# Another order for the opening of an attention-then-FFN kernel: v cast, copies, phis and transposes moved between engines

## The chip, the cores and the metric

The kernel runs on one core of one Trainium2 chip. The time is device microseconds of one execution, from start to end; a verdict is made on the median of several executions. TensorE (PE) multiplies, VectorE (DVE), ScalarE (ACT) and GpSimd (POOL) work elementwise, and SyncE (SP) issues most of the loads and stores. GpSimd also issues the DMAs that cast the weights to bf16 on their way in. Each engine works through its own instructions in the order written.

## The reference

```python
# attention: q, k, v are (8, 8, 576, 64) float32
theta = np.pi / 2.0 * pos / S
phi(x) = concatenate([relu(x) * cos(theta), relu(x) * sin(theta)])   # 64 -> 128
kv  = einsum('bhsf,bhsd->bhfd', phi(k), v);   z = phi(k).sum(axis=2)
num = einsum('bhsf,bhfd->bhsd', phi(q), kv);  den = einsum('bhsf,bhf->bhs', phi(q), z) + 1e-06
x = (num / den)            # heads side by side: 4608 tokens x 512
# gated FFN on x
xn  = x / sqrt(mean(x * x) + 1e-06) * rms_g
out = (silu(xn @ w_gate) * (xn @ w_val)) @ w_out          # 512 -> 1536 -> 512, float32
```

## The kernel before

The instruction order is written by hand (`manual_schedule`); semaphores are added between engines. Each of the eight batches gives 512 tokens, a block of four tiles of 128, and 64 left-over tokens that are gathered in a ninth block. In the steady state of blocks 1 to 8, `gval_step` multiplies one of twelve 128-wide slices of the gate and value weights with a block (L546), ScalarE takes the silu (L555), VectorE the product (L561), and `out_step` multiplies with `w_out` (L566). The attention of the next batches is slotted between these steps.

The change concerns the opening, where batch 0 has nothing to hide behind. For it tokens and heads lie differently: the loads bring `k`, `q` and `v` of batch 0 as four head pairs r = 0 to 3 of nine token columns j each.

1. `k_phi` writes phi(k) (`kpm`) by halves of the pairs, LOW = (0, 2) and HIGH = (2, 4), and `q_phi` writes a tile of phi(q) (`qp`) in two parts, part 0 the cosine half and part 1 the sine half, each as two instructions, i = 0 and 1 (L252 on ScalarE, L254 on VectorE).
2. `v_cast` turns `v` into bf16 with a column of ones (`vvm`), pair by pair (L337 on ScalarE, L339 on VectorE).
3. `kvz_mm` (L386) multiplies them, LOW into `psG[1]` and `psV[1]`, HIGH into `psA`; `kvz_copy` brings the products to SBUF (`kvzs`).
4. `q_tr_pe` (L321) transposes a q tile on TensorE into `psO`, `q_tr_evac` copies it out (`qpT`).
5. `nd_half` (L431) and `nd_pe` (L414) multiply q tiles with `kvzs`; `nd_post_half` (L450 to L454) and `nd_post` (L465 to L469) divide, giving a tile of x (`xt`).
6. `x_sq` (L480) takes the mean square on ScalarE and its power of -1/2 on GpSimd (`rs`, L485). `x_norm` (L507) makes the normalised tile `xn` in one VectorE instruction. For tile 0 alone this is split in three: `x_gain` (L494, twice, half a tile each, needs no `rs`) and `x_scale` (L500).
7. `x_tr_pe` (L532) transposes `xn`, `x_tr_evac` copies it to `xnT`, and `open_ffn` (L692) does the first six slices of the FFN of block 0, first for token tile 0 (columns 0 to 128), then tile 1, then 2 and 3.

`filler` (L593) multiplies zeros into an unused bank, to keep TensorE busy. The weight loads are issued by `weight_slice` (L236) on GpSimd, gate and value in turn; here w0 to w9 are `weight_dmas[0]` to `[9]` (w0, w1: columns 0 to 256; w2, w3: to 512; w4, w5: to 768; then 384 columns each). `k` of batch 1 is loaded in two pieces: one pair (288 KB) among the first loads, the other three after w5 has landed. `q` of batch 1 waits for w8, and the second part of `w_out` for that q.

In this order the lines after L653, where LOW is multiplied, set what each engine does up to the start of the FFN at L719.

Of the kernel before, what the change touches and what calls it, by code (L numbers as in the profile page):

```python
# [9 lines left out]
FP32 = mybir.dt.float32  # L10
BF16 = mybir.dt.bfloat16
AF = mybir.ActivationFunctionType
ALU = mybir.AluOpType
# [13 lines left out]
def kernel(  # L27
# [11 lines left out]
    nc = tc.nc  # L39
    B, H, S, D = q.shape  # L40
    DM = H * D
    DFF = moe_w_gate.shape[1]
    P = 128
# [10 lines left out]
    three = ctx.enter_context(tc.tile_pool(name="three", bufs=3))  # L54
# [13 lines left out]
    NJ = 9  # L68
# [5 lines left out]
    def load_kv(which, b, r0=0, r1=4, j0=0, j1=NJ):  # L74

        key = (which, b)
        if key not in raw:
            raw[key] = (two if which == "k" else one).tile(
                [P, 4, NJ * D], FP32, name=f"r{which}", tag=f"r{which}"
            )  # L80
        src = {"k": k, "v": v}[which]
        return nc.sync.dma_start(
            out=raw[key][:, r0:r1, j0 * D : j1 * D],
            in_=src[b, 2 * r0 : 2 * r1, :, :]
            .rearrange("h s d -> (h s d)")
            .rearrange("(r p n) -> p r n", p=P, n=NJ * D)[:, :, j0 * D : j1 * D],
        )
# [80 lines left out]
    load_kv("v", 0, 3, 4, 0, 5)  # L168
    load_kv("v", 0, 3, 4, 5, NJ)
    load_q_tokens(4, NJ)  # L170
    load_kv("k", 1, 0, 1)
    nc.scalar.preload_act_table(AF.Silu)
    gb = one.tile([P, DM], FP32, name="gb")

# [60 lines left out]
    def weight_slice(w_sb, w_dram, c0, c1):  # L235
        return nc.gpsimd.dma_start(  # L236
            out=w_sb[:, :, c0:c1],
            in_=w_dram[:, c0:c1].rearrange("(t p) n -> p t n", p=P),
        )
# [41 lines left out]
            src = flat[:, 2048:2304].rearrange("p (i d) -> p i d", d=D)  # L281
        phi(eng, kp_of(b)[:, 8 * c : min(8 * c + 8, 36), o], src, f(c))

    def q_phi(eng, b, c, part):
        o = slice(0, D) if part == 0 else slice(D, F)
        f = cos_of if part == 0 else sin_of
        if (b, c) not in qp_tiles:
            qp_tiles[(b, c)] = four.tile(
                [P, H if c < 4 else 4, F], BF16, name="qp", tag="qp" if c < 4 else "qpt"
            )  # L290
        if b == 0:
            for i in range(2 if c < 4 else 1):
                j = 2 * c + i
                f = cos_of if part == 0 else sin_of
                phi(
                    eng, qp_tiles[(b, c)][:, 4 * i : 4 * i + 4, o],
                    raw[("q", 0)][:, :, j * D : (j + 1) * D], f(5 + j),
                )
            return
        src = view4(raw[("q", b)], c) if c < 4 else raw[("qt", b)][:, :, :]  # L300
        phi(eng, qp_tiles[(b, c)][:, :, o], src, f(c))
# [15 lines left out]
    def q_tr_pe(b, c, bank):  # L317
        t = qp_tiles[(b, c)]
        dst = bank.bitcast(BF16).rearrange("p (h s) -> p h s", s=P)
        for h in range(H if c < 4 else 4):  # L320
            nc.tensor.transpose(dst[:, h, :], t[:, h, :], ident[:, :])  # L321

    def q_tr_evac(eng, b, c, bank, heads=(0, 8)):
        h0, h1 = heads if c < 4 else (0, 4)
        if b == 0:
            src = bank.bitcast(BF16).rearrange("p (i h s) -> p h i s", i=2, h=H)
            copy(
                eng, q_dst(b, c)[:, h0:h1, :].rearrange("p h (i s) -> p h i s", i=2),
                src[:, h0:h1, :, :],
            )  # L330
            return
        dst = bank.bitcast(BF16).rearrange("p (h s) -> p h s", s=P)
        copy(eng, q_dst(b, c)[:, h0:h1, :], dst[:, h0:h1, :])
# [7 lines left out]
    def v_cast(eng, b, r0=0, r1=4, j0=0, j1=NJ):  # L341
        copy(
            eng, vvm[b % 2][:, r0:r1, j0:j1, 0:D],
            raw[("v", b)][:, r0:r1, j0 * D : j1 * D].rearrange("p r (j d) -> p r j d", d=D),
        )
# [34 lines left out]
    def kvz_mm(b, banks, rs=(0, 4)):  # L380

        for r in range(*rs):
            for j in range(NJ):
                for c in range(2):
                    lo = 64 * c
                    nc.tensor.matmul(  # L386
                        banks[c][:, r * E : (r + 1) * E],
                        lhsT=kp_main[b][lo : lo + 64, j, r, :],
                        rhs=vvm[b % 2][lo : lo + 64, r, j, :],
                        start=(j == 0), stop=(j == NJ - 1),  # L390
                    )
# [4 lines left out]
    def kvz_copy(eng, b, c, bank, rs=(0, 4)):  # L396
        if (b, c) not in kvzs:
            kvzs[(b, c)] = three.tile([P, 4 * E], BF16, name="kvzs", tag=f"kvzs{c}")
        lo, hi = rs[0] * E, rs[1] * E
        copy(eng, kvzs[(b, c)][:, lo:hi], bank[:, lo:hi])  # L400
# [7 lines left out]
    def nd_pe(b, j, pst):  # L408

        o = headview(pst)  # L410
        for h in range(H):
            g, i = h // 4, h % 4
            if j < 4:
                nc.tensor.matmul(  # L414
                    o[:, g, i, :], lhsT=qpT[(b, 0)][:, h, j * P : (j + 1) * P],
                    rhs=kvz_of(b, h), start=True, stop=True,
                )
            else:
                for bb in (b - 1, b):
                    lo = 64 * (bb % 2)  # L420
                    r, c = (h // 2, h % 2) if bb == 0 else (i, g)
                    nc.tensor.matmul(
                        o[lo : lo + 64, g, i, :],
                        lhsT=qpT[(bb, 1)][:, r, 64 * c : 64 * c + 64],
                        rhs=kvz_of(bb, h), start=True, stop=True,
                    )
# [49 lines left out]
    def x_sq(b, j):  # L476
        xt = x_of[(b, j)]
        scr = one.tile([P, DM + 1], BF16, name="scr", tag="scr")
        ms = four.tile([P, 1], FP32, name="ms", tag="ms")
        nc.scalar.activation(  # L480
            out=scr[:, :], in_=xt[:, 0 : DM + 1], func=AF.Square,
            scale=1.0 / math.sqrt(DM), accum_out=ms[:, :],
        )
        rs = four.tile([P, 1], FP32, name="rs", tag="rs")
        nc.gpsimd.tensor_tensor(out=rs[:, :], in0=ms[:, :], in1=mhalf[:, :], op=ALU.pow)  # L485
        rs_of[(b, j)] = rs

    xn_of = {}
    xg = three.tile([P, DM], FP32, name="sg", tag="sg")

    def x_gain(b, j, g):

        c = slice(g * DM // 2, (g + 1) * DM // 2)
        nc.vector.tensor_tensor(  # L494
            out=xg[:, c], in0=x_of[(b, j)][:, c], in1=gb[:, c], op=ALU.mult
        )

    def x_scale(b, j):
        xn = four.tile([P, DM], BF16, name="xn", tag="xn")
        nc.vector.tensor_scalar(  # L500
            out=xn[:, :], in0=xg[:, :], scalar1=rs_of[(b, j)][:, :], scalar2=None, op0=ALU.mult
        )
        xn_of[(b, j)] = xn

    def x_norm(b, j):
        xn = four.tile([P, DM], BF16, name="xn", tag="xn")
        nc.vector.scalar_tensor_tensor(  # L507
# [83 lines left out]
    def filler(n, bank):  # L591
        for _ in range(n):
            nc.tensor.matmul(bank, lhsT=warm[:, 0:P], rhs=warm[:, :], start=True, stop=True)  # L593
# [25 lines left out]
    def gval_slice(c0, c1):  # L619
        weight_dmas.append(weight_slice(wg, moe_w_gate, c0, c1))  # L620
        weight_dmas.append(weight_slice(wv, moe_w_val, c0, c1))
# [3 lines left out]
        weight_dmas[0].ins, first_v.ins.name, SYNC_DEP, reason="weights after v"  # L625
    )
    gval_slice(256, 512)
    gval_slice(512, 768)

    wo_dmas = []  # L630

    def wo_load(i):
# [18 lines left out]
    low_banks = [psG[1][:, :], psV[1][:, :]]  # L651
    high_banks = [psA[:, c, :] for c in range(2)]
    kvz_mm(0, low_banks, LOW)  # L653
    kvz_copy(A, 0, 0, low_banks[0], LOW)
    kvz_copy(A, 0, 1, low_banks[1], LOW)
    v_cast(V, 0, 3, 4, 0, 5)
    v_cast(V, 0, 3, 4, 5, NJ)
    kvz_mm(0, high_banks, (2, 3))
    nd_half(0, 0, 0, psV[0])
    nd_post_half(0, 0, 0, psV[0])  # L660
    x_gain(0, 0, 0)
    q_tr_evac(A, 0, 1, psO[0][:, :], (0, 4))
    kvz_mm(0, high_banks, (3, 4))
    kvz_copy(A, 0, 0, high_banks[0], HIGH)
    kvz_copy(A, 0, 1, high_banks[1], HIGH)
    filler(1, idle)
    nd_half(0, 0, 1, psO[1])
    nd_post_half(0, 0, 1, psO[1])
    q_tr_evac(A, 0, 1, psO[0][:, :], (4, 8))
    q_phi(A, 0, 2, 1)  # L670
    x_sq(0, 0)
    nd_pe(0, 1, psA)
    nd_post(0, 1, psA)
    x_gain(0, 0, 1)
    q_phi(A, 0, 2, 0)
    x_sq(0, 1)
    gval_slice(768, 1152)
    gval_slice(1152, 1536)
    filler(7, psV[1][:, :])
    q_tr_pe(0, 2, psO[0][:, :])  # L680
    x_scale(0, 0)

    def open_ffn(pair, steps, c0, c1, first=0, parts=(0, 1)):

# [26 lines left out]
    for half, (eng, bank) in enumerate(((A, psG[1]), (V, psV[1]))):  # L711
        part = (2 * half, 2 * half + 2)
        x_tr_pe(0, 0, bank[:, :], part)
        x_tr_evac(eng, 0, 0, bank[:, :], part)
    q_phi(A, 0, 3, 1)
    q_tr_evac(A, 0, 2, psO[0][:, :])
    x_norm(0, 1)
    q_phi(V, 0, 3, 0)
    open_ffn(0, (0, 1), 0, 128)  # L719
    x_tr_pe(0, 1, psV[1][:, :])  # L720
    x_tr_evac(V, 0, 1, psV[1][:, :])
    q_tr_pe(0, 3, psO[1][:, :])
    nd_pe(0, 2, psA)
    nd_post(0, 2, psA)
    q_tr_evac(A, 0, 3, psO[1][:, :])
    x_sq(0, 2)
    wo_load(0)
    open_ffn(0, (0, 1), 128, 256)
# [45 lines left out]
        for f, args in slots.get((blk, n), none())[where]:  # L774
            f(*args)

    d = load_kv("k", 1, 1, 4)
    tc.add_manual_dep(d.ins, weight_dmas[5].ins.name, SYNC_DEP, reason="after most weights")
    gate_q = load_q(1)
    tc.add_manual_dep(  # L780
# [233 lines left out]
```

## Time and profile before

| | us |
|---|---|
| median of 4 runs | 326.57 (326.34 to 326.83) |
| the profiled execution's own time | 326.38 |
| its span in the trace | 324.6 |
| TensorE busy | 316.3 (97%) |
| VectorE busy | 184.5 (57%) |
| ScalarE busy | 173.8 (54%) |
| GpSimd busy | 38.9 (12%) |

The span is the trace from its first to its last record; 1.78 us of the execution lie outside it. Times in the views are microseconds from the start of the span. A row of the timeline gives start, duration, engine, line, operation, output and inputs, a count if rows are merged, and in brackets the idle time before it with what ended it. A row of the chain of waits gives start, duration and instruction.

### The profile page before, as it was taken

The numbers are of one execution on the slowest core, as the hardware profiler recorded it, in microseconds if no ns is written. First come the engines' busy times: TensorE is split into PE (matmuls) and PEld (weight loads), VectorE is DVE, ScalarE is ACT, GpSimd is POOL, SyncE is SP. The second block draws the span as 40 slices with busy tenths as digits, with TensorE's granted clock in tenths as the row PEclk, the third lists the DMA queues.
The fourth block names the chain that finished last, engine by engine and source line by source line (L and its number), as shares of the span: only waits on it lengthen the run. The fifth ranks groups of instructions, "written<-read, shape, count | busy, mean of one in ns | idle before, by whom it ended". The sixth has DMA issues, their size and how long they took to land.

```text
span 324.6 us, 6131 instructions
## 1 busy us (share of the span) xinstructions
PE 316.3 (97%) x2249; PEld 162.6 (50%) x2284; DVE 184.5 (57%) x398; ACT 173.8 (54%) x351; POOL 38.9 (12%) x85
## 2 busy tenths in 40 slices
PE   8899999999999999999999999999999999999995
PEld 3588465554445444554454445444544444444443
DVE  5975768787656765578267745772577133203410
ACT  6974875965665556645555466555644333223321
POOL 4660202001110110011001120120011000000000
PEclk9999999999999999999999999999999999999999
DMA  7999999898799776999598879966621400020014
GB/s 274 289 198 254 298 220 347 213 168 205 156 247 270 182 204 152 238 168 184 174 212 209 149 225 208 184 168 205 139 41 33 131 32 0 24 107 0 1 33 99
DMA packets 89378, 53.90 MB, mean 166 GB/s; under 512 B 56322, under 2 KB 81922, under 8 KB 89347
## 3 DMA queue, kind: packets, MB, share of 16 engines
q1 hardware_dynamic: 82304, 48.65, 59.3%
q0 software_dynamic: 6880, 4.72, 9.9%
q8 instruction: 18, 0.29, 0.4%
q10 hardware_dynamic: 162, 0.13, 0.2%
q14 instruction: 14, 0.11, 0.1%
HBM read 37.75 MB, written 9.44 MB: 145 GB/s over the span
## 4 chain that ended last, share of the span: by engine, by line
PE 89%; DVE 5%; ACT 2%; issue 1%; DMA 1%; POOL 0%; DVEq 0%
PE psC L566 26%; PE psV L546 26%; PE psG L546 26%; PE psA L414 2%; PE psA L370 2%; DVE kpm L254 1%; PE psG L566 1%; DMA rk<-in_k_dram 1%; DVE qp L254 1%; PE psO L692 1%; PE psG L692 1%; PE psV L692 1%; DVE hT L561 1%; ACT kpm L252 1%; PE psA L386 1%
## 5 line engine op out<-in xcount | busy, mean ns | idle before, releaser
L561 DVE TENSOR_TENSOR hT<-psV,sg 128x512 bf16<-128x512 f32 x102 | 70.2, 689 | 96.0 <-PE psV L546 71.1
L555 ACT ACTIVATE sg<-psG 128x512 f32<-128x512 f32 x102 | 60.6, 594 | 64.5 <-PE psG L546 63.2
L546 PE MATMUL psV<-xnT,wv 128*128 128x512 bf16 (+1 forms) x365 | 92.1, 374 | 0.4
L546 PE MATMUL psG<-xnT,wg 128*128 128x512 bf16 (+1 forms) x352 | 90.8, 374 | 0.7
L566 PE MATMUL psC<-wo,hT 128*128 128x512 bf16 x382 | 88.2, 379 | 0.7
L546 PEld LDWEIGHTS <-wv 128*128 128x128 bf16 x416 | 40.6, 98 | 47.4
L566 PEld LDWEIGHTS <-hT 128*128 128x128 bf16 x420 | 40.2, 98 | 46.7
L546 PEld LDWEIGHTS <-wg 128*128 128x128 bf16 x416 | 38.5, 98 | 40.8 <-DVE xnT L339 0.4
L485 POOL TENSOR_TENSOR rs<-ms,mhalf 128x1 f32<-128x1 f32 x36 | 19.8, 549 | 188.9 <-ACT scr L480 188.9
L337 ACT COPY osb<-psC 128x512 f32<-128x512 f32 (+1 forms) x33 | 19.1, 579 | 43.1 <-PE psC L566 42.4
L507 DVE SCALAR_TENSOR_TENSOR xn<-xt,rs,gb 128x512 bf16<-128x512 f32 x35 | 26.4, 754 | 16.4 <-POOL rs L485 16.3
L480 ACT ACTIVATE scr<-xt 128x513 bf16<-128x513 f32 x36 | 22.8, 635 | 23.6 <-DVE xt L469 23.6
L252 ACT ACTIVATE kpm<-rk,tab 128x256 bf16<-128x256 f32 (+2 forms) x58 | 28.2, 545 | 1.8 <-DMA rk<-in_k_dram 1.8
L469 DVE TENSOR_TENSOR xt<-psA,rec 128x512 f32<-128x512 f32 x35 | 24.2, 691 | 1.2
L252 ACT ACTIVATE qp<-rq,tab 128x512 bf16<-128x512 f32 (+1 forms) x37 | 23.7, 661 | 0.0
L254 DVE TENSOR_SCALAR kpm<-rk,tab 128x128 bf16<-128x128 f32 (+2 forms) x64 | 20.4, 378 | 2.3 <-DMA rk<-in_k_dram 2.3
L254 DVE TENSOR_SCALAR qp<-rq,tab 128x512 bf16<-128x512 f32 (+1 forms) x37 | 16.3, 460 | 0.0
L414 PEld LDWEIGHTS <-qpT 128*128 128x128 bf16 x248 | 11.7, 98 | 6.7 <-issue 0.3
L414 PE MATMUL psA<-kvzs,qpT 128*128 128x65 bf16 x248 | 12.8, 194 | 0.3
L546 PE MATMUL psG<-xnt_tail,wg 128*128 128x512 bf16 x48 | 12.3, 379 | 0.1
L546 PE MATMUL psV<-xnt_tail,wv 128*128 128x512 bf16 x47 | 12.1, 379 | 0.0
L339 DVE CAST vvm<-rv 128x1024 bf16<-128x1024 f32 (+4 forms) x16 | 10.5, 680 | 0.0
(99 smaller groups left out, 183.4 us busy)
## 6 DMA issues: line engine op xcount, KB each, us to landing
out_dram<-osb SPq DMA_DIRECT2D x28, 256.0 KB, 2.6
rk<-in_k_dram SPq DMA_DIRECT2D x20, 256.0 KB, 3.3
rq<-in_q_dram SPq DMA_DIRECT2D x20, 256.0 KB, 3.5
rv<-in_v_dram SPq DMA_DIRECT2D x16, 256.0 KB, 3.3
rq<-in_q_dram SPq DMA_DIRECT2D x2, 1024.0 KB, 9.0
out_dram<-osb SPq DMA_DIRECT2D x14, 128.0 KB, 3.2
rv<-in_v_dram SPq DMA_DIRECT2D x3, 576.0 KB, 8.0
wo<-in_moe_w_out_dram POOLq DMA_DIRECT2D x4, 384.0 KB, 7.2
```

What stands on the lines that cost most here:

```text
L252: nc.scalar.activation(out=out_ap, in_=in_ap, func=AF.Relu, scale=scale)
L254: eng.tensor_scalar(out=out_ap, in0=in_ap, scalar1=scale, scalar2=0.0, op0=ALU.mult, op1=ALU.max)
L337: nc.scalar.copy(out=o, in_=i)
L414: nc.tensor.matmul(o[:, g, i, :], lhsT=qpT[(b, 0)][:, h, j * P : (j + 1) * P], rhs=kvz_of(b, h), start=True, stop=True,)
L469: nc.vector.tensor_tensor(out=xt[:, 0:DM].rearrange("p (b h d) -> p b h d", b=2, d=D), in0=o[:, :, :, 0:D], in1=rec[:, :, :].unsqueeze(3). ...
L480: nc.scalar.activation(out=scr[:, :], in_=xt[:, 0 : DM + 1], func=AF.Square, scale=1.0 / math.sqrt(DM), accum_out=ms[:, :],)
L485: nc.gpsimd.tensor_tensor(out=rs[:, :], in0=ms[:, :], in1=mhalf[:, :], op=ALU.pow)
L507: nc.vector.scalar_tensor_tensor(out=xn[:, :], in0=x_of[(b, j)][:, 0:DM], scalar=rs_of[(b, j)][:, :], in1=gb[:, :], op0=ALU.mult, op1=ALU. ...
L546: nc.tensor.matmul(pst[bank][:, cols[0] : cols[1]], lhsT=w[:, t, n * P : (n + 1) * P], rhs=x[:, t, cols[0] : cols[1]], start=(t == 0), sto ...
L555: nc.scalar.activation(out=sg[:, :], in_=psG[bank][:, :], func=AF.Silu)
L561: nc.vector.tensor_tensor(out=hTs[blk][:, n, :], in0=psV[bank][:, :], in1=sg[:, :], op=ALU.mult)
L566: nc.tensor.matmul(bank, lhsT=hTs[blk][:, n, j * P : (j + 1) * P], rhs=wo[:, n, :], start=(n == 0), stop=(n == NNT - 1),)
```

## The change

All of it lies in the opening.

- The last v pair is cast by ScalarE (columns 0 to 5) and VectorE (5 to 9); before, VectorE cast both parts.
- HIGH is multiplied in one go, ahead of the first `nd_half`, and its two products are copied by VectorE instead of ScalarE.
- The two halves of `x_gain` and `x_scale` go; tile 0 is normalised by `x_norm`.
- Of q tile 2, part 0 goes from ScalarE to GpSimd, and the two instructions of part 1 are set apart on ScalarE. Of q tile 3, part 1 goes to VectorE and part 0 to ScalarE, both ahead of the FFN; before, part 0 was VectorE's and stood after `x_norm(0, 1)`.
- `q_tr_pe(0, 3)` stands ahead of the FFN's first matmuls, and its copy right behind that of tile 2.
- w4 is issued after the first `rs`, w5 after the second; before, both were issued together with w0 to w3. GpSimd's two phis stand between w3 and the first `rs`.
- `k` of batch 1 is loaded in one piece after w5; the early pair is gone.
- The fillers: before one, later seven; now six and two.

```diff
-    load_kv("k", 1, 0, 1)
...
-    def q_phi(eng, b, c, part):
+    def q_phi(eng, b, c, part, subs=(0, 1)):
...
-            for i in range(2 if c < 4 else 1):
+            for i in subs if c < 4 else (0,):
...
-    xg = three.tile([P, DM], FP32, name="sg", tag="sg")
-
-    def x_gain(b, j, g):
-
-        c = slice(g * DM // 2, (g + 1) * DM // 2)
-        nc.vector.tensor_tensor(
-            out=xg[:, c], in0=x_of[(b, j)][:, c], in1=gb[:, c], op=ALU.mult
-        )
-
-    def x_scale(b, j):
-        xn = four.tile([P, DM], BF16, name="xn", tag="xn")
-        nc.vector.tensor_scalar(
-            out=xn[:, :], in0=xg[:, :], scalar1=rs_of[(b, j)][:, :], scalar2=None, op0=ALU.mult
-        )
-        xn_of[(b, j)] = xn
...
     gval_slice(256, 512)
-    gval_slice(512, 768)
...
     kvz_mm(0, low_banks, LOW)
+    v_cast(A, 0, 3, 4, 0, 5)
+    v_cast(V, 0, 3, 4, 5, NJ)
+    kvz_mm(0, high_banks, HIGH)
     kvz_copy(A, 0, 0, low_banks[0], LOW)
     kvz_copy(A, 0, 1, low_banks[1], LOW)
-    v_cast(V, 0, 3, 4, 0, 5)
-    v_cast(V, 0, 3, 4, 5, NJ)
-    kvz_mm(0, high_banks, (2, 3))
+    kvz_copy(V, 0, 0, high_banks[0], HIGH)
+    kvz_copy(V, 0, 1, high_banks[1], HIGH)
+    q_tr_evac(A, 0, 1, psO[0][:, :], (0, 4))
     nd_half(0, 0, 0, psV[0])
     nd_post_half(0, 0, 0, psV[0])
-    x_gain(0, 0, 0)
-    q_tr_evac(A, 0, 1, psO[0][:, :], (0, 4))
-    kvz_mm(0, high_banks, (3, 4))
-    kvz_copy(A, 0, 0, high_banks[0], HIGH)
-    kvz_copy(A, 0, 1, high_banks[1], HIGH)
-    filler(1, idle)
     nd_half(0, 0, 1, psO[1])
     nd_post_half(0, 0, 1, psO[1])
     q_tr_evac(A, 0, 1, psO[0][:, :], (4, 8))
-    q_phi(A, 0, 2, 1)
+    q_phi(G, 0, 2, 0)
+    q_phi(A, 0, 2, 1, (0,))
     x_sq(0, 0)
+    weight_dmas.append(weight_slice(wg, moe_w_gate, 512, 768))
     nd_pe(0, 1, psA)
     nd_post(0, 1, psA)
-    x_gain(0, 0, 1)
-    q_phi(A, 0, 2, 0)
+    q_phi(A, 0, 2, 1, (1,))
+    q_phi(V, 0, 3, 1, (0,))
+    x_norm(0, 0)
+    q_phi(V, 0, 3, 1, (1,))
     x_sq(0, 1)
+    weight_dmas.append(weight_slice(wv, moe_w_val, 512, 768))
     gval_slice(768, 1152)
     gval_slice(1152, 1536)
-    filler(7, psV[1][:, :])
+    q_phi(A, 0, 3, 0)
+    filler(6, psV[1][:, :])
     q_tr_pe(0, 2, psO[0][:, :])
-    x_scale(0, 0)
+    filler(2, psV[1][:, :])
...
         x_tr_evac(eng, 0, 0, bank[:, :], part)
-    q_phi(A, 0, 3, 1)
+    q_tr_pe(0, 3, psO[1][:, :])
     q_tr_evac(A, 0, 2, psO[0][:, :])
     x_norm(0, 1)
-    q_phi(V, 0, 3, 0)
+    q_tr_evac(A, 0, 3, psO[1][:, :])
     open_ffn(0, (0, 1), 0, 128)
     x_tr_pe(0, 1, psV[1][:, :])
     x_tr_evac(V, 0, 1, psV[1][:, :])
-    q_tr_pe(0, 3, psO[1][:, :])
     nd_pe(0, 2, psA)
     nd_post(0, 2, psA)
-    q_tr_evac(A, 0, 3, psO[1][:, :])
     x_sq(0, 2)
...
-    d = load_kv("k", 1, 1, 4)
+    d = load_kv("k", 1)
```

## The prediction

> **What bounds the kernel.** I read the page's busy times and chain first, then the chain of waits from 13.9 to 21 us, then the timeline there.
>
> ```profile
> PE 316.3 (97%) x2249; PEld 162.6 (50%) x2284; DVE 184.5 (57%) x398; ACT 173.8 (54%) x351; POOL 38.9 (12%) x85
> PEclk9999999999999999999999999999999999999999
> PE 89%; DVE 5%; ACT 2%; issue 1%; DMA 1%; POOL 0%; DVEq 0%
> ```
>
> TensorE is the bound at full clock. Only the opening runs on other engines. The windows view gives TensorE 10.00 us busy from 20 to 30 us and 29.57 of the 30 after, so what the opening gains by about 20 us stays gained unless something that doesn't move with TensorE (a transfer) is then late. The chain of waits into the FFN:
>
> ```profile
> 14.71 0.72 ACT scr L480 x2
> ...
> 16.92 0.56 POOL rs L485
> ...
> 17.51 0.75 DVE xn L507
> 18.26 0.82 DVE qp L254 x2
> 19.08 0.14 issue
> 19.22 0.38 PE psO L321 x4
> 19.60 0.25 PE psA L414 x8
> 19.85 0.22 PE psG L692 x4
> ```
>
> The FFN of token tile 1 waits for q tile 3: its phi sits on VectorE behind `xn` of tile 1, then come its transposes and the product of q tile 2. In the timeline:
>
> ```profile
> 16.12 0.48 DVE L500 TENSOR_SCALAR xn<-sg,rs 128x512 bf16<-128x512 f32 x1
> ...
> 16.98 0.37 ACT L337 COPY xnT<-psG 128x256 bf16<-128x256 bf16 x1
> ...
> 17.41 0.38 PE L692 MATMUL psG<-xnT,wg 128*128 128x128 bf16 x4 [0.35 <-ACT xnT L337]
> ...
> 18.99 0.40 DVE L339 COPY xnT<-psV 128x512 bf16<-128x512 bf16 x1
> ...
> 19.44 0.41 PE L414 MATMUL psA<-kvzs,qpT 128*128 128x65 bf16 x8
> ...
> 19.68 0.39 PE L692 MATMUL psG<-xnT,wg 128*128 128x128 bf16 x4
> ```
>
> FFN tile 0 starts at 17.41, tile 1 at 19.68, 2.27 later. From 19.68 TensorE doesn't stop. I forecast that second number.
>
> [...] The trace has GpSimd casts of 64x256 at 0.39 to 0.75. [...]
>
> ```profile
> 121.28 1.20 POOL L339 CAST vvt<-rv 64x256 bf16<-64x256 f32 x2
> 121.36 0.86 DVE L507 SCALAR_TENSOR_TENSOR xn<-xt,rs,gb 128x512 bf16<-128x512 f32 x1 [2.09 <-POOL rs L485]
> 122.14 0.49 DVE L254 TENSOR_SCALAR kpm<-rk,tab 128x256 bf16<-128x256 f32 x1
> ```
>
> Alone the two last take 0.74 and 0.34. [...]
>
> **Part by part**, in start times.
>
> *v pair 3, HIGH, copies.* ScalarE's casts of pairs 0 and 2 end at 11.47 and it then waits 0.27 for LOW. A 128x320 cast fits nearly there: between 128x576 (0.67) and 128x1152 (1.14) the slope is 0.82 ns an element, so 0.46, from 11.40 to 11.86; the copies of LOW slip from 11.74 to 11.78. VectorE's 128x256 (0.38) runs from 11.54. HIGH's last 18 products then start at 11.92, not 12.41, and end at 12.38. VectorE's two copies: 12.44, and 12.65 to 12.94 (a following instruction starts some 0.08 before the end). They stand before the division of half 0, whose first instruction moves from 12.51 to 12.86. Dropping the first `x_gain` (0.34 of slot) pays for that: half 1 is divided at 14.00 to 14.42 instead of 14.20 to 14.62. **x tile 0: 0.20 earlier.**
>
> *Tile 0.* scr to `rs` takes 0.81, `rs` 0.57: scr at 14.51, `rs` 15.32 to 15.89. `x_norm` (0.75) replaces `x_scale` (0.48): 0.27 longer. The second `x_gain` was hidden in the wait for `rs` and gains nothing. `xn` ends at 16.67, against 16.60. Its copy on ScalarE: x tile 1 is ready at 15.45 (was 15.65), scr then 15.56, 0.63 of slot, two phis of q tile 3 0.83, so free at 17.02; the transposes are ready at 17.05. FFN tile 0: **17.48, 0.07 later**.
>
> *A collision.* VectorE's new phi (0.34, q tile 3) stands at 15.37, on top of this `rs`. None of the views shows a phi beside an `rs`. Bounds: 0 [...] to 0.36 (one waits for the other whole). I take 0.10, below the 0.15 beside a cast, since `rs` touches one element a partition. FFN tile 0: 17.58.
>
> *q tile 3.* Its transposes fill TensorE's wait before the FFN (ScalarE's phis end by 17.18, transposes by 17.46). Nothing stands between `x_norm` of tile 1 (17.4 to 18.17) and the copy of its transposes: after FFN tile 0, 0.91 as before, transposes plus copy 0.86, handover 0.06: FFN tile 1 is 1.83 after tile 0, not 2.27. q tile 2's copy (ScalarE, 17.32 to 18.32) and product fit in between, q tile 3's copy ends at 19.23, well before its product at about 20.7. FFN tile 1: 17.58 + 1.83 = **19.41, 0.27 earlier**.
>
> *GpSimd.* The phis start after w3, about 12.95 (q landed before 13.71, when ScalarE reads it without waiting). At 0.5 each, 0.4 to 1.2 as bounds, they end by 14.0 (13.8 to 15.4); `rs` needs GpSimd at 15.32, q tile 2's transposes need the phis when ScalarE's last phi ends, 15.65. Covered. w4 (0.77) behind the first `rs` holds the second from 16.4 to 16.6; VectorE could use it only from 17.4.
>
> *Transfers.* Issue of w4 moves from 12.90 to about 15.9, w5 from 13.63 to 17.2. The DMA view by single microseconds has the weights at 0.19 to 0.20 MB/us from 13 to 26 us, so w0 to w3 (1.05 MB) keep the queue busy till about 17.4, starting up to 0.7 sooner because the 288 KB of k no longer precede them. A software transfer issued at 38.39 moves nearly all its bytes after 40, so w4 flows from about 17.6 and w5 follows: gap 0.2. w4 is needed at 22.1, w5 at 23.3. Before, SP held k of batch 1 for w5 until 22.56:
>
> ```profile
> SPq L82 <- DMA wv<-in_moe_w_val_dram: 16.6, 1, 16.6
> ```
>
> So w5 landed 1.1 before its use at 23.66; I expect it at 22 (to 23). k is now 1152 KB, not 864 (8.3 from issue to landing); it moved at 0.23 MB/us, so 1.3 longer: lands at 31.6 to 32.6, needed by ScalarE at 33.1. Covered, by the least margin here. `q`, `v` and `w_out` of batch 1 had 2 us or more. Fillers total eight both times.
>
> *Sum.* -0.20 + 0.27 + 0.10 - 0.44 = -0.27. The profiled execution, 326.38 (span 324.6 and 1.78 around it), would be 326.11. It lay 0.19 below the median: 326.57 - 0.27 = **326.3**.
>
> **Rivals.** About 0.2%, 0.65 us, is what a measurement here tells from no change.
>
> 1. *The remaining waits close too* (0.2). TensorE idles 0.51 between 16 and 20 (2.00 - 1.65 and 2.00 - 1.84). If x tile 0 comes sooner than I add up and this goes as well: 325.8; with no collision 325.7. For: every engine is off its queue at 15 us. Against: the chain scr, `rs`, `x_norm` is serial.
> 2. *GpSimd's phis hold up `rs`* (0.1): slower. The point is 1.2 us each; above it every excess counts twice, on FFN tile 0. At 2.0 each: 1.6 late, 327.9. For: no such operation is in the trace. Against: casts at 0.39 to 0.75.
> 3. *A transfer is late* (0.06): w5 by over a microsecond or k by 0.5 to 1.5. ScalarE then stands before the next silu: 326.8 to 327.8.
> 4. *The clock drops* (0.04): between 14.8 and 17.5 TensorE has only two fillers and transposes. [...]
> 5. *The collision takes all of the gain* (0.12 of the 0.6 below): 326.5 to 326.7.
>
> **Numbers.** My case with rival 5 (0.6) stays within 0.2%; faster 0.2 is rival 1; slower 0.2 is rivals 2 to 4. The unknown costs alone give 326.0 to 326.7; reaching into rivals 1 and 2 the range is 325.6 to 327.9.
>
> **What would show it.** Right: division of half 1 at 14.0 (first row 13.6), `rs` at 15.3, FFN tile 0 near 17.5, tile 1 near 19.4 with an idle 0.4 before it put down to VectorE's `xnT`, no phi between `xn` and that copy, step six of the FFN at 29.9. Wrong: `rs` released by GpSimd's phi, FFN tile 0 after 18, TensorE waiting at 22 to 24 for w4 or w5 or at 33 to 36 behind ScalarE's `kpm`, PEclk below 9.

## The result, and the profile after

The changed kernel takes 327.21 us in the median of 39 runs (326.17 to 329.09), the kernel before 326.50 beside it (59 runs, 326.23 to 327.21). The ratio is 1.0025, with a 95% interval of 1.0018 to 1.0033: slower by a quarter of a per cent, where 0.27 us less was forecast. The lowest times of the two are alike; the changed kernel's times reach much higher. The profiled execution took 327.31 us, with a span of 325.5, 0.9 longer than before.

The same lines of the page as before (busy times, clock, chain by engine):

```profile
PE 316.1 (97%) x2249; PEld 162.4 (50%) x2284; DVE 183.9 (56%) x397; ACT 173.1 (53%) x348; POOL 42.5 (13%) x87
PEclk9999999999999999999999999999999999999999
PE 87%; DMA 4%; POOL 2%; ACT 2%; DVE 2%; SPq 1%; issue 1%; ACTq 0%
```

TensorE has as much to do as before, at full clock. What the chain has gained is DMA (1% to 4%) and GpSimd (0% to 2%), on which the prediction's main case put no path. GpSimd's part lies in the opening. The chain of waits there (start, duration, what):

```profile
13.58 2.32 POOL qp L253 x2
15.89 0.59 POOL rs L484
...
16.51 0.77 DVE xn L490
...
18.16 0.29 PE psG L676 x4
...
19.38 0.43 DVE xnT L338
...
19.86 0.38 PE psG L676 x4
```

and the timeline of the same stretch:

```profile
10.39 0.94 POOL L235 DMA_DIRECT2D wg<-in_moe_w_gate_dram  x1 [6.05 <-DMA rv<-in_v_dram]
...
13.58 2.32 POOL L253 TENSOR_SCALAR qp<-rq,tab 128x256 bf16<-128x256 f32 x2
...
14.68 0.64 ACT L479 ACTIVATE scr<-xt 128x513 bf16<-128x513 f32 x1 [0.81 <-DVE rec L464]
...
15.53 0.51 DVE L253 TENSOR_SCALAR qp<-rq,tab 128x256 bf16<-128x256 f32 x1
16.51 0.76 DVE L490 SCALAR_TENSOR_TENSOR xn<-xt,rs,gb 128x512 bf16<-128x512 f32 x1 [0.46 <-POOL rs L484]
...
18.07 0.38 PE L676 MATMUL psG<-xnT,wg 128*128 128x128 bf16 x4
...
19.86 0.38 PE L676 MATMUL psG<-xnT,wg 128*128 128x128 bf16 x4 [0.27 <-DVE xnT L338]
```

GpSimd's two phis take 2.32 us, start at 13.58 because w0 could be issued only at 10.39 (the first `v` landed later than in the profile of before, where w0 starts at 9.77), and end at 15.9. The first `rs` starts at 15.82; it was forecast at 15.32, 0.81 behind a `scr` at 14.51. As `scr` started at 14.68, the phis hold `rs` by 0.33. FFN tile 0 starts at 18.07 instead of 17.58. Tile 1 follows 1.79 later, as forecast (1.83), but at 19.86, which is 0.18 later than before and not 0.27 earlier.

At the first steps of the FFN in the steady state 0.12 of this lag is left (30.25 against 30.13). The chain of waits shows a second piece near 97 us:

```profile
89.61 3.24 SPq L121
...
92.90 4.32 DMA rv<-in_v_dram
...
97.28 0.96 POOL vvt L338
...
98.28 1.25 PE psA L369 x36
```

The last rows of `v` of batch 3 land at 97.22. GpSimd casts them (`vvt`), and TensorE, which has begun batch 3's products with `v`, stops for them until 98.28. In the timeline of the kernel before the cast starts 0.68 earlier, and the product runs at 97.74 without a wait:

```profile
96.60 0.94 POOL L339 CAST vvt<-rv 64x256 bf16<-64x256 f32 x2 [6.06 <-DMA rv<-in_v_dram]
```

and in that of the changed kernel:

```profile
97.28 1.41 POOL L338 CAST vvt<-rv 64x256 bf16<-64x256 f32 x2 [6.60 <-DMA rv<-in_v_dram]
```

TensorE loses 0.42 us more here. SP is held 3.24 us at one issue of this `v` (0.43 before). That this makes the rows late is not shown: in E5, E7 and E12 below the wait is there too, and the same issue takes 0.42 to 0.43.

The third piece lies behind the last instruction. The last issue of the program, on ScalarE's queue, in the timeline of the kernel before:

```profile
321.35 0.50 ACTq L981 DMA_DIRECT2D out_dram<-osb  x1
```

in that of the changed kernel, and the last packet of its trace in the DMA view by half microseconds (packets, MB, share of the window):

```profile
321.89 0.50 ACTq L963 DMA_DIRECT2D out_dram<-osb  x1
```

```profile
q14 instruction: 1, 0.01, 4.5%
```

This last packet is of kind "instruction" and lies in the window 325 to 325.5; in the kernel before the packet lies in the window 323 to 323.5. From ScalarE's last issue to the end of the trace it takes 3.25 us before and 3.61 after. Together the pieces explain the difference of the spans: 0.12, 0.42 and 0.36 are 0.90.

### The profile page after: what moved, and what is told of

Its sections match the earlier page's. It is cut to its first block, busy times and chain, and to the rows that moved or that the text cites. A ratio compares the mean times of both kernels' runs of the same rounds, so it can differ in the third digit from the quotient of the medians.

```text
span 325.5 us, 6127 instructions
## 1 busy us (share of the span) xinstructions
PE 316.1 (97%) x2249; PEld 162.4 (50%) x2284; DVE 183.9 (56%) x397; ACT 173.1 (53%) x348; POOL 42.5 (13%) x87
## 4 chain that ended last, share of the span: by engine, by line
PE 87%; DMA 4%; POOL 2%; ACT 2%; DVE 2%; SPq 1%; issue 1%; ACTq 0%
PE psC L549 25%; PE psV L529 25%; PE psG L529 25%; DMA rv<-in_v_dram 4%; PE psA L413 2%; PE psA L369 2%; PE psG L549 2%; PE psG L676 1%; PE psV L676 1%; PE psO L676 1%; SPq L121 1%; ACT kpm L251 1%; POOL qp L253 1%; PE psA L385 1%; PE psV L320 1%
## 5 line engine op out<-in xcount | busy, mean ns | idle before, releaser
L490 DVE SCALAR_TENSOR_TENSOR xn<-xt,rs,gb 128x512 bf16<-128x512 f32 x36 | 27.2, 755 | 16.8 <-POOL rs L484 16.8
L251 ACT ACTIVATE qp<-rq,tab 128x512 bf16<-128x512 f32 (+1 forms) x35 | 22.8, 669 | 0.1
L338 DVE CAST vvm<-rv 128x1024 bf16<-128x1024 f32 (+3 forms) x15 | 10.0, 689 | 0.1
```

Source lines behind the costliest of these rows:

```text
L251: nc.scalar.activation(out=out_ap, in_=in_ap, func=AF.Relu, scale=scale)
L490: nc.vector.scalar_tensor_tensor(out=xn[:, :], in0=x_of[(b, j)][:, 0:DM], scalar=rs_of[(b, j)][:, :], in1=gb[:, :], op0=ALU.mult, op1=ALU. ...
```

## The experiments

Each was run beside the kernel before, whose median was 326.54 (E0 to E3), 326.43 (E4 to E7), 326.44 (E8 to E11) and 326.57 (E12 to E14); each of these groups ran on one chip. Three suspects have letters. **P**: GpSimd's phis hold the first `rs`. **W**: w4 and w5 are issued behind the two `rs`, so w5 lands late. **F**: SP issues one transfer fewer, and the end of the program is longer. At the start F was not seen; its place was taken by **D** (`k` and `q` of batch 1 come late), and the wait near 97 us was called **L**.

**E0, the changed kernel again.** No edit.

> The changed kernel once more, for a second trace and more times. The runs so far spread from 326.2 to 329.1 us against 326.2 to 327.2 before, and the one trace has three candidates. Theory P (GpSimd's two phis, 1.16 us each, hold the first rs): the FFN of token tile 1 starts near 19.9 us again in this trace, and everything after it runs at the pace of before. Theory D (loads of batch 1 late): q of batch 1 is issued near 33.2 us instead of 30.9, and TensorE loses time at 40 to 46 us in slow executions. Theory L (a later wait, for v of batch 3 near 97 us): 0.4 us or more is lost there. Each theory expects a median of 327.2; which of the three places the trace shows late tells them apart.

Measured: 327.39 (326.24 to 330.28), ratio 1.003 (1.0015 to 1.0044). The profile caught an execution of 328.59 us. In the waits from 23 to 28 us (total, times, longest):

```profile
PEld L676 <- DMA wv<-in_moe_w_val_dram: 1.4, 1, 1.4
PE psO L676 <- DMA wv<-in_moe_w_val_dram: 1.2, 1, 1.2
```

and in TensorE's timeline:

```profile
25.50 1.05 PE L676 MATMUL psO<-xnT,wv 128*128 128x256 bf16 x8 [1.20 <-DMA wv<-in_moe_w_val_dram]
```

TensorE stands before the products with w5, which the kernel before starts at 23.71. Here nothing is lost at 97 us. So executions of one kernel lose their time in different places.

**E1, the early piece of `k` restored.**

```diff
+    load_kv("k", 1, 0, 1)
...
-    d = load_kv("k", 1)
+    d = load_kv("k", 1, 1, 4)
```

> The changed kernel with k of batch 1 in two pieces again: the first pair among the first loads, the rest after w5. Theory D: the load after w5 is 288 KB smaller, q of batch 1 is issued about 1.3 us sooner (near 32), the spread upwards shrinks and the median falls to 326.3 to 326.7. Theory P: the opening is untouched, FFN tile 1 near 19.9, median 327.1 to 327.3.

Measured: 326.89 (325.81 to 328.33), ratio 1.0015 (1.0005 to 1.0025). Half a microsecond comes back, to between the two expectations, but the times still reach high. The lowest is 0.47 below the lowest of the kernel before in that group (326.28): the opening can be ahead when nothing else is late.

**E2, GpSimd's phi moved to ScalarE.**

```diff
-    q_phi(G, 0, 2, 0)
+    q_phi(A, 0, 2, 0, (0,))
...
+    q_phi(A, 0, 2, 0, (1,))
```

> The changed kernel with part 0 of q tile 2 on ScalarE again, in its idle time before and after the first mean square, and not on GpSimd. Theory P: GpSimd is free when the first mean square ends, so rs starts at about 15.3 to 15.4 and not 15.8, FFN tile 1 at 19.4, median 0.3 to 0.6 lower (326.6 to 326.9). w4 and w5 are issued sooner with it, w5 by up to 1 us, so theory D expects something too: q of batch 1 issued 0.5 to 1 us sooner and the spread smaller, but not gone. If neither median nor spread moves, both are wrong and theory L is left.

Measured: 326.82 (326.45 to 327.52), ratio 1.001 (1.0002 to 1.0018). The first `rs` starts at 15.46. It looked as if P were 0.57 us; E12 says otherwise.

**E3, the kernel before with `k` of batch 1 in one piece behind w5.**

> The kernel before with one edit of the change: k of batch 1 in one piece after w5. Theory D: q of batch 1 is issued 0.5 to 1.5 us later than the 30.9 of before, and the spread grows upwards, median 0 to 0.4 above before. Theory P: nothing, within 0.1 us of before (326.5).

Measured: 327.20 (326.73 to 328.46), ratio 1.0018 (1.0007 to 1.0029). The trace does not bear D out: up to 260 us TensorE is not behind the kernel before (0.06 ahead), and the last issue comes 0.05 earlier, at 321.30. Yet the span is 0.4 longer, all of it behind that issue, with the instruction packet in the window 324.5 to 325. From this came F.

**E4, as E3 but with `k` in its two pieces, both behind w5**, so SP issues as many transfers as in the kernel before.

```diff
-    d = load_kv("k", 1)
+    d = load_kv("k", 1, 0, 1)
...
+    load_kv("k", 1, 1, 4)
```

> The kernel before, with k of batch 1 loaded behind w5 as in the changed kernel, but in its two pieces (rows 0 to 1, then 1 to 4), so that SP issues as many transfers as before. Theory F (end of program): with k in one piece SP issues one transfer fewer, and the trace then has its last instruction packet some 3 us instead of 1.5 us behind ScalarE's last issue, and ends 3.6 to 3.7 instead of 3.25 us behind it; if that is all that the late k costs, this kernel shows 3.25 us there and runs at 326.5, like the kernel before. Theory D (k, q and v of batch 1 come late): it is as late here as with one piece, so 327.2. Half of each: 326.8.

Measured: 326.56 (326.24 to 327.13), ratio 1.0004 (0.9996 to 1.0012). `k` is as late as in E3 and the loss is gone. **D falls, F stands.** The end takes 3.3 us again, and the last packet comes in the window 323 to 323.5.

**E5, the same two late pieces in the changed kernel.**

> The changed kernel with k of batch 1 still behind w5, but issued in two pieces. Theory F: the trace ends 3.25 us behind ScalarE's last issue instead of 3.6, and the time falls by 0.4, from 327.4 to 327.0; what is left over the kernel before is the late first rs and late w5. Theory D: no change, 327.4.

Measured: 327.00 (326.25 to 329.30), ratio 1.002 (1.0009 to 1.0032), the end 3.23: F is 0.4 of the loss, as expected. In this profile the first `v` landed early (w0 at 9.75), so the phis did not hold `rs`: it started at 15.18, 0.81 behind its `scr`, and FFN tile 1 at 19.18, half a microsecond ahead of the kernel before. TensorE then waited for w5:

```profile
23.88 1.05 PE L676 MATMUL psO<-xnT,wv 128*128 128x256 bf16 x8 [0.56 <-DMA wv<-in_moe_w_val_dram]
```

By 27 us the lead had turned into a lag of 0.17, and at 97 us another 0.54 went. Being early in the opening was worth nothing here, as w5 was not there.

**E6, all three undone**: the phi as in E2, the early piece of `k` as in E1, and w4 and w5 behind w3:

```diff
     gval_slice(256, 512)
+    gval_slice(512, 768)
...
-    weight_dmas.append(weight_slice(wg, moe_w_gate, 512, 768))
...
-    weight_dmas.append(weight_slice(wv, moe_w_val, 512, 768))
```

> The changed kernel with GpSimd's phi back on ScalarE, w4 and w5 issued with w0 to w3 again, and the first piece of k of batch 1 back in the opening. Left of the change: the last v pair cast by two engines, its copies on VectorE, x_norm in place of x_gain and x_scale, q tile 3 transposed ahead of the FFN. If P, the late w5 and F are all that the change loses: the first FFN tile starts at 17.4 to 17.6, the second 1.8 us later, all later work 0.2 to 0.4 us ahead of the kernel before, and the time is 326.1 to 326.3 with no long upper tail. If the parts left cost something themselves: 326.5 or more.

Measured: 326.17 (325.96 to 327.67), ratio 0.9998 (0.9989 to 1.0007). The opening is as expected: FFN tile 0 at 17.55, tile 1 at 19.34, all later work 0.34 ahead. It is the earliest opening of the seven profiles with the phi on ScalarE (tile 1 at 19.34 to 19.68). The median is 0.26 below that of the kernel before, but 6 of the 14 times lie above 326.4, and the interval doesn't tell it from no change.

**E7, the kernel before with W alone** (w4 and w5 behind the two `rs`).

> The kernel before with one thing of the change: w4 and w5 issued on GpSimd's queue behind the first and second rs instead of directly behind w3. Theory W (the transfers of the FFN's weights have no room left): w5 lands 1 us later, at 23.5, TensorE waits for it in some executions and not in others, so the lowest time stays within 0.1 of the kernel before and the median rises by 0.2 to 0.5, with times above 328. If w4 and w5 have room: 326.5 with the spread of the kernel before.

Measured: 326.71 (326.35 to 327.76), ratio 1.001 (1.0001 to 1.0018). SP issued `k`, which waits for w5, at 23.13 instead of 22.56 in the kernel before. There was no wait for w5 (this kernel reaches it later), but the wait near 97 us was there, at 0.42. So that wait can come with W alone, without P or F.

**E8, the changed kernel with W alone** of the three: E2 with `k` in two late pieces.

> The changed kernel without GpSimd's phi (it is on ScalarE) and with k of batch 1 in two late pieces: of the three suspects P (phi on GpSimd), F (one issue fewer on SP, longer end) and W (w4 and w5 behind the two rs), W alone is left, with the parts of the change that seem to gain. If the three add up: 326.4 to 326.5, which is 0.4 below the run with only the phi moved back (326.82), 3.25 us from ScalarE's last issue to the end, and 0.2 to 0.3 above the run that undoes all three (326.17). If F and the phi are the same loss counted twice: 326.8.

Measured: 327.14 (326.16 to 328.97), ratio 1.002 (1.0009 to 1.003). A miss: W alone, in this order, costs about as much as the whole change. The profile caught one of the fastest executions (326.16), which has neither the wait for w5 nor the one near 97 us, so the slow ones of this kernel were not seen in a trace.

**E9, E8 with w4 and w5 behind w3**: none of the three suspects is left, with `k` still late.

> The changed kernel with the phi on ScalarE, w4 and w5 issued with w0 to w3, and k of batch 1 still late but in two pieces. By F and by the run of the kernel before with the same two late pieces (326.56 against 326.43), a late k costs at most 0.1 itself, so this is as fast as the run that also loads k early: 326.2 to 326.3. If the early piece of k is worth something in the changed order: 326.5.

Measured: 326.32 (326.18 to 326.81), ratio 0.9993 (0.9985 to 1.0001). Against E8 on the same chip: W is 0.8 in the median and 2.2 in the highest time. In TensorE's timeline FFN tile 1 follows tile 0 by 1.79, but starts only 0.07 ahead of the kernel before:

```profile
17.82 0.38 PE L676 MATMUL psG<-xnT,wg 128*128 128x128 bf16 x4
...
19.61 0.38 PE L676 MATMUL psG<-xnT,wg 128*128 128x128 bf16 x4 [0.27 <-DVE xnT L338]
```

A part of why w5 is late is seen in the DMA view of 20 to 22 us. The software queue, which carries only GpSimd's weights (packets, MB, share of the window of one engine), in E9:

```profile
q0 software_dynamic: 719, 0.39, 140.8%
```

in the kernel before:

```profile
q0 software_dynamic: 606, 0.39, 134.6%
```

and in the changed kernel:

```profile
q0 software_dynamic: 593, 0.30, 124.8%
```

In the eight profiles with w4 and w5 early (before, E3, E4, E6, E9 to E11, E14) this queue moves 0.34 to 0.40 MB in these two microseconds, in the nine with them behind the `rs` 0.28 to 0.32. Against the kernel before that is a matter of larger packets (some 640 bytes against 510), but against E9 there are fewer packets too. The queue doesn't run empty in between: w0 to w3 are 1.05 MB, of which 0.90 have moved by 18 us; w4 is asked for at 16.43 and w5 at 17.91. Why it moves less is not shown.

Nor is this all of it. w0 to w5 are 1.57 MB. By 22 us the queue had moved 1.57 MB in the changed kernel and 1.59 in E13 below, but SP's issue of `k`, which waits for w5, came at 22.87 and 24.40. So the bytes ahead of a transfer don't give its landing: with as many moved, w5 was ready 0.9 later in one profile and 2.4 in the other. What decides that was not found.

**E10, the changed kernel with w4 and w5 behind w3 and the phis still on GpSimd** (`k` in two late pieces): P alone, made later by the six issues ahead of the phis.

> The changed kernel with k in two late pieces and w4 and w5 issued directly behind w3, so that GpSimd's two phi come behind six weight issues. Theory P: the phi start about 1.5 us later, at 14.4 to 15.1, end 2.3 us later at 16.7 to 17.4, the first rs follows at once, 1.4 to 2.1 us later than in the kernel before (15.3), the first FFN tile starts at 19.0 to 19.6, the second 1.8 later, and the time is 327.6 to 328.0. w5 is no longer late, so the spread is small. If the phi do not hold the path: 326.4.

Measured: 328.82 (327.94 to 329.81), ratio 1.0067 (1.0048 to 1.0086). The chain of waits:

```profile
15.08 2.31 POOL qp L253 x2
17.39 0.55 POOL rs L484
```

`rs` starts 1.9 later than in E9 and the span is 1.9 longer: in this profile a late `rs` is paid in full, as w5 is not late. The median lies 2.5 above E9's, which is more than expected; the slower executions were not seen in a trace. With the phis on GpSimd ahead of `rs`, asking for w4 and w5 early did worse here than asking late (328.82 against 327.00 in E5, on two chips).

**E11, the kernel before with `v` of batch 1 in one piece.**

```diff
-    load_kv("v", 1, *LOW)
-    load_kv("v", 1, *HIGH)
+    load_kv("v", 1)
```

> The kernel before with v of batch 1 loaded in one piece instead of two: again one issue fewer on SP, with k untouched and early. Theory F: 3.65 instead of 3.25 us from ScalarE's last issue to the end of the trace, and 326.8 to 326.9 instead of 326.45. If the longer end belongs to the late k and not to the number of issues: 3.25 us and 326.45.

Measured: 326.94 (326.83 to 327.79), ratio 1.0015 (1.0009 to 1.0022), the end 3.75. `k` is untouched, and the loss and the late packet are there. So in E3 and E11 F came with one issue fewer on SP, whether the load was `k` or `v`.

**E12 to E14** ask again for W's price, which E2 (next to nothing) and E8 (0.8) had left open. E12 is E2 again.

> The changed kernel with only GpSimd's phi moved to ScalarE, once more (k of batch 1 in one late piece, w4 and w5 behind the two rs). If W's price differs between chips and executions: as far above its twin with w4 and w5 early (e14) as e13 was above its own in the earlier call, that is 327.2 to 327.6, with times above 328. If k in one late piece keeps W free of cost: 326.8 and nothing above 327.6, as before.

E13 is E8 again.

> The same with k in two late pieces, once more. If W costs 0.8 in this order: 327.1 again, with times up to 329, and 0.4 under e12 if the longer end comes on top of W. If W's price was an accident of one call: 326.4.

E14 has the phi on ScalarE, w4 and w5 behind w3 and `k` in one late piece: F alone.

> The changed kernel with the phi on ScalarE and w4 and w5 issued with w0 to w3; k in one late piece. Of the three suspects F alone is left. Theory F: 0.4 to 0.5 above the same kernel with k in two pieces (326.32), so 326.7 to 326.8, with a narrow spread and 3.65 us from ScalarE's last issue to the end of the trace.

Measured: E12 327.30 (326.38 to 330.92), ratio 1.003 (1.0016 to 1.0043); E13 326.97 (326.10 to 329.09), ratio 1.0016 (1.0004 to 1.0028); E14 326.68 (326.46 to 327.55), ratio 1.0006 (0.9998 to 1.0014). E12 against E14, one edit on one chip: W is 0.6. E12 against E13: F is 0.3. E14 against E9, on two chips: F is 0.36. The profile of E13 has the wait for w5, at 22 to 29 us:

```profile
PE psO L677 <- DMA wv<-in_moe_w_val_dram: 0.7, 1, 0.7
```

and that of E12 the wait near 97 us (0.42). E12 is the very kernel of E2 and is slower by 0.5, with a far wider spread: W's price differs from execution to execution and between the groups of runs. What decides it is not settled.

## Why the prediction was wrong

**The opening's largest term was right; that its sum came out in E6 is in part luck.** FFN tile 1 starts 1.79 to 1.80 after tile 0 in all twelve profiles with the changed opening (forecast 1.83), and 2.27 to 2.31 after it in the five with the opening of before, so -0.44 holds. E6 has tile 0 at 17.55 (17.58), tile 1 at 19.34 (19.41) and all later work 0.34 ahead of the kernel before (0.27). But three differences nearly cancel there:

- Half 1 was divided at 13.80, 0.20 ahead of the forecast. In the twelve profiles this comes at 13.80 to 14.45 (14.02 to 14.20 in the five). It follows VectorE's cast of the last `v` piece by 2.4 to 2.5, and in E0, E10 and E12 that cast waits 0.17 to 0.22 for its data, in none of the five. The prediction had the times of one trace in it. VectorE's two copies of HIGH, 0.29 each in the forecast by an estimate of the author's, took 0.28 and 0.29 in after.
- The collision, +0.10, was nothing: where GpSimd has no phi, VectorE's phi took 0.34 beside `rs` and `rs` 0.57, as each does alone. In the changed kernel the phi took 0.51, but VectorE then waited 0.46 for `rs` anyway.
- Against these, the phi moved back to ScalarE makes ScalarE's copy of `xnT` late: tile 0 starts 1.82 to 1.83 behind its `xn` in the seven profiles with the phi there, and 1.55 to 1.56 in after, E0, E1 and E5, which is 0.27 less.

The seven have tile 1 at 19.52 on average, the five at 19.61: 0.08 ahead, not 0.27. In the medians E6 and E9 lie 0.26 and 0.12 below the kernel before beside them.

**"GpSimd. ... At 0.5 each ... Covered" failed in two terms.** The price: 1.16 us apart in the timeline (1.19 in the groups), near the upper bound of 0.4 to 1.2, where the 0.5 was an estimate from another operation, GpSimd's casts of 64x256 (0.39 to 0.75 in the trace of before). The start: 12.95 was w0's start in one profile plus 3.18. In the profiles of after, E0 and E5 the phis start 3.18 to 3.19 behind w0 as well, but w0 is released by the first `v`, which let it start at 9.75, 10.39 and 10.69. The point of rival 2, 1.2 us each, was right for 12.95 only; 0.6 later it is 0.9 each. So the phis hold `rs` in some executions, by 0.33 and 0.34 in after and E0, and not in others, E1 and E5. The size of P in the median could not be told apart: with W there E5 (327.00) lies between E8 and E13 (327.14 and 326.97). Either the phis mostly don't hold `rs`, as in E5's own profile, or a late `rs` hides behind a late w5. Behind six weight issues `rs` starts 1.9 later, and without W that is paid in full (E10).

**"w5 follows: gap 0.2 ... at 22 (to 23)" is the step that cost most.** The bytes of w0 to w5 were set into a queue running at 0.19 to 0.20 MB/us to the end of w9. With the issues later the queue ran at 0.15 from 20 to 22, and w5 was ready up to 2.4 behind the point at which its bytes should have moved (E13). SP's issue of `k`, released by w5, shows the landing:

```profile
SPq L82 <- DMA wv<-in_moe_w_val_dram: 18.0, 1, 18.0
```

In the profiles with w4 and w5 early (before, E3, E4, E6, E9 to E11, E14) that issue comes at 21.91 to 22.71; with them late at 22.54 to 25.47. The use was at 23.7 and had been moved forward by the change itself. Rival 3 named this, by w5 over a microsecond late and 326.8 to 327.8, but got 0.06 of the chance, because one landing in one trace was read as a fixed time. A loss near 97 us was in no part of the prediction. The wait there appears in 4 of the 9 profiles with w4 and w5 late (after, E5, E7, E12) and in none of the 8 with them early; with one profile a kernel that is a small count, and how it gets from 25 us to 97 was not followed.

**`k` was "Covered, by the least margin here", and it was.** E4 costs nothing that can be measured. What the edit does cost was not in the list of what a moved load brings: the number of issues on SP. The end lasts 3.61 to 3.75 us in the seven kernels that issue one fewer (after, E0, E2, E3, E11, E12, E14) and 3.23 to 3.30 in the nine others and the kernel before, with nothing between. That is 0.3 to 0.6 us in the median (E3 and E4, E0 and E5, E14 and E9).

**The clock did not drop** (PEclk 9 throughout, 1.0 granted in the profiled execution) and TensorE's other waits did not close, so rivals 1 and 4 are out. That this opening could lower the clock was the author's assumption; no trace here shows it. Rival 5 is out too: beside `rs` alone the phi took 0.34, as it does alone.

In sum, three steps failed: the start and price of GpSimd's phis, w5's landing, and the number of SP's issues, which the prediction put at nothing. From the changed kernel: F 0.4, and W with whatever of P it hides 0.7 (E5 to E9, on two chips), against a gain of about 0.2 that is left when all are removed. Each measured against the kernel before beside it, E6 and E9 beat the changed kernel by 0.8 to 1.0 us in the median; over the kernel before they gain 0.1 to 0.3, which the intervals don't separate from nothing.

## What to carry to other kernels

Before an operation is put into a queue that also issues transfers, ask what its issues wait for and how far the landings behind it differ between executions: a margin read in one trace is one draw (w0 started at 9.75 in E5, 10.39 in after and 10.69 in E0), and a gain ahead of a transfer can go into a wait for it, as in E5 (tile 1 half a microsecond ahead, then 0.56 of wait for w5). Here w5 asked for later also landed later (`k` issued behind it at 22.54 to 25.47 against 21.91 to 22.71), in a queue with bytes left to move, and the bytes ahead of it didn't give its landing: with 1.57 and 1.59 MB moved by 22 us `k` was issued at 22.87 and 24.40. When a sum comes out right, look at its terms: here three errors nearly cancelled. And when the times differ but TensorE's own starts don't, look behind the last instruction (0.4 us in E3).

## What the runs showed of the hardware that was not expected

- With one issue fewer on SP the program's end took some 0.4 us longer (3.61 to 3.75 against 3.23 to 3.30): its last packet, of kind "instruction", came 3.3 to 3.6 us behind the last issue instead of 1.9 to 2.3. That it follows the count is shown for one fewer (E3, E4, E11); why it does is not, and other counts were not tried.
- GpSimd's tensor_scalar with two operations, 128x256 from float32 to bf16, took 1.16 us in after (VectorE alone 0.34, ScalarE some 0.42 of slot). A VectorE phi wholly beside it took 0.34 in E10; one that stood over its end and the start of `rs` took 0.51 in after and E0.
- Between 20 and 22 us the software queue moved 0.34 to 0.40 MB in the profiles with six weight transfers asked for early, and 0.28 to 0.32 with four and two.
- One 256 KB weight transfer, w5, landed between 22.54 and 25.47 in nine profiles of kernels that issue it behind the second `rs`.
- The same kernel ran at 326.82 and at 327.30 in the medians on two chips (E2 and E12), while the kernel before stayed within 0.14.
